# A second softmax taken in halves in every step, in a kernel whose whole order is a table

## The chip, the cores and the metric

The kernel runs on one core of a Trainium2 chip, in float32. The metric is the device time of one execution in microseconds (us). Five kinds of engine share the work: PE (TensorE, matrix products; PEld is its loading of weights), DVE (VectorE), ACT (ScalarE), POOL (GpSimd) and SP (SyncE, which here issues every transfer). Sixteen DMA engines move data between the chip's memory (HBM) and the on-chip buffers.

## The reference, cut to what matters

```python
# q, k, v: (8 batches, 8 heads, 576, 64); p: (8, 8, 32, 64)
def sm_attn(qq, kk, vv):
    s = scale * np.matmul(qq, kk.transpose(0, 1, 3, 2))
    a = np.exp(s - np.max(s, axis=-1, keepdims=True))
    a = a / (np.sum(a, axis=-1, keepdims=True) + 1e-09)
    return np.matmul(a, vv)
p_packed = sm_attn(p, k, v)               # first softmax, over 576 keys
x = sm_attn(q, p_packed, p_packed)        # second softmax, over 32 pack rows
# x becomes (4608 tokens, 512); phi: (512, 32 slots); w1: (8, 512, 1024); w2: (8, 1024, 512)
logits = x @ phi
d = softmax(logits over tokens);  slot_input = d.T @ x       # 8 experts x 4 slots
slot_out[e] = np.maximum(slot_input[e] @ w1[e], 0.0) @ w2[e]
c = softmax(logits over slots);   out = c @ slot_out
```

## The kernel before, in words

**Steps.** The attention is done in 8 steps: step i holds one pair of batches (dd = i // 2) and one half of the heads (g = i % 2, four heads). A step goes from the scores of the pack queries (s1) through the first softmax (mx1, e1), its transposes (ap, copied by apc), the product with v (m, scaled by ppa and pp), the transpose of the result (pt, copied by ptc), the product with phi (mp, copied by mm), the transposes of q (qp, copied by qc), the second scores (s2), the second softmax (mx2 the maximum over 32 pack rows, sb the subtraction, e2 the exponential, z2 the sum, rc the reciprocal of the sum, n2 the normalisation) and the transposes of its probabilities (a2p, copied by a2c) to the routing logits (lg). kt is DVE's 32x32 transposition of k. Names that begin with f and g, and rt, rb, gt, gs, sa, keep a running softmax over tokens and gather the slot inputs after every second step. Then come the experts' two layers (weights streamed from HBM) and the output, whose 36 tiles of 128 tokens are stored as they are made: the first 16 tiles by left and right halves of their 512 columns, the others whole.

**Order.** Nothing is scheduled by itself: a long string, ORDER, lists tokens `name.i.j@bank:engine` (step i, part j, PSUM bank, a for ACT, v for DVE, p for POOL), and each token calls the function f_name. Every engine works its instructions off in that order. A transfer's place on SP's queue follows from it too.

**Parts of the second softmax.** The scores of a step are two halves by the parity of the head (576 of 1152 elements per partition each). `mx2.i.2` and `sb.i.2` take both halves at once, `mx2.i.0` and `.1` one; e2, z2, rc and n2 take part 0 (all), 6 or 7 (one parity). On DVE z2 is one reduction; on POOL it is one addition and two shorter ones, and rc then begins with a short reduction on DVE. Before the change steps 0 to 5 use the whole and steps 6 and 7 halves.

**Loads.** All loads are issued by SP in one fixed list into a ring of 30 x 4096 bytes per partition. ALLOW holds them back: the load of index ALLOW[k] waits until 194 + 256 k products' worth of PE work is done (a product counts 4, a transpose 2; a pause of PE's counter, not of time). The load of a late chunk of weights, the only one into the tile `a` (PLACE's letter "x"), waits for the end of the attention, and the ring's later loads wait for the first expert layer to free their places.

**Stores.** `ends_a` lists after which left-half tiles a transfer is sent:

```python
    def tiles(t0, t1, x):
        ...
            ends = (ends_a, ends_b)[x]
            if t + 1 in ends:
                send(max(n for n in (0, *ends) if n <= t), t + 1, x)
```

Of the kernel before, what the change touches and what calls it, by code (L numbers as in the profile page):

```python
# [34 lines left out]
a2p.0.1@3 a2c.0.0:a rz.2.0 kt.3.3 ap.2.2@2 e2.1.0 ap.2.0@0 apc.2.2:v s1.3.0@4 a2c.0.1:a z2.1.0:p
s1.3.1 apc.2.0:a a2c.0.2:a m.2.0@2 mx1.3.0 m.2.1 m.2.2 e1.3.0 rc.1.0 e1.3.1 lg.0.0@1 n2.1.0:v
ppa.2.1 ap.3.1@0 ra.3.0 ap.3.0@7 ppa.2.0 apc.3.1:a ap.3.2@6 pp.2.1 apc.3.0:a a2p.1.2@5 kt.4.1
a2p.1.0@0 a2c.1.2:a apc.3.2:v a2p.1.1@7 a2c.1.0:a rz.3.0 m.3.0@4 pp.2.0 a2c.1.1:a kt.4.3 lg.0.1
kt.4.2 pt.2.0 f1.0.0 m.3.1 ptc.2.1:a ptc.2.0:a kt.4.0 f2.0.0 m.3.2 f3.0.0 f5.0.0 mp.2.0 fd.0.0
ppa.3.1 f6.0.0 mm.2.0:v ppa.3.0 pp.3.1 gr.0.0@6 pp.3.0 gz.0.0 fl.0.0 s2.2.0@1 rt.0.1:v rt.0.0:a  # L40
s2.2.1 qp.3.2@0 mx2.2.2 pt.3.0 qc.3.2:a gt.0.0 ptc.3.1:a ptc.3.0:v qp.3.5@0 rb.0.0 sb.2.2 mp.3.0
qc.3.5:a gs.0.0 mm.3.0:a qp.3.1@0 qp.3.3@5 qc.3.1:a sa.0.0 e2.2.0 qp.3.0@4 qp.3.4@7 qc.3.0:v
s1.4.0@0 qc.3.3:a z2.2.0:p s1.4.1 qc.3.4:a kt.5.0 kt.5.2 s2.3.0@5 mx1.4.0 s2.3.1 kt.5.1 e1.4.1
qp.4.5@4 mx2.3.2 e1.4.0 qc.4.5:a ap.4.2@0 ra.4.0 rc.2.0 qp.4.3@1 apc.4.2:a ap.4.1@4 sb.3.2 n2.2.0:p
qc.4.3:a qp.4.1@3 ap.4.0@0 apc.4.1:a qp.4.4@2 qp.4.2@1 qc.4.1:a qc.4.4:a kt.5.3 e2.3.0 s1.5.0@4
rz.4.0 apc.4.0:v s1.5.1 qc.4.2:a kt.6.0 z2.3.0:p a2p.2.0@0 mx1.5.0 a2p.2.2@1 a2c.2.0:a m.4.0@2
# [1207 lines left out]
```

## Time and profile before

| | before |
|---|---|
| median of 3 runs | 198.3 us (197.76 to 199.04) |
| the profiled execution | 198.95 us |
| its span | 196.8 us |
| PE busy | 167.2 us (85%) |
| DVE busy | 124.1 us (63%) |
| ACT busy | 89.7 us (46%) |
| POOL busy | 35.7 us (18%) |
| HBM read, written | 62.46 MB, 9.44 MB |

The span is the time from the first to the last event of the profiled execution; the 2.15 us by which the execution is longer lie around it. The attention's eight steps fill the first 135 us, the experts' weights and products the stretch to 167 us, the output the rest. Transfers run from the first microseconds to the end.

### The profile page before, as it was taken

How to read it: one execution, taken by the hardware profiler on the slowest of the kernel's cores; microseconds unless marked ns; L12 is line 12 of the kernel's file. 1: busy time of each engine (PE TensorE's matmuls, PEld its weight loads, DVE VectorE, ACT ScalarE, POOL GpSimd, SP SyncE). 2: the span in 40 equal slices, each digit the busy share in tenths (PEclk: the TensorE clock that was granted, in tenths of full speed). 3: DMA queues.
4: the chain of work that ended last, by engine and by line, in shares of the span. 5: the costliest groups of instructions: out<-in, count | busy, mean ns of one | idle time of the engine just before them, and what ended most of it. 6: DMA issues, size and time to landing. Idle time of an engine off the chain costs nothing.

```text
span 196.8 us, 6563 instructions
## 1 busy us (share of the span) xinstructions
PE 167.2 (85%) x2841; PEld 108.9 (55%) x2841; DVE 124.1 (63%) x261; ACT 89.7 (46%) x229; POOL 35.7 (18%) x61
## 2 busy tenths in 40 slices
PE   7978986999999999999999989687999997979100
PEld 4454574786777778597797867433333232448000
DVE  1657639797848999969746899745575111569300
ACT  4084273696526589575357367322021001459300
POOL 7400000544000572000403670403000000000000
PEclk9999999999999999999999999999999999999955
DMA  5999999699999999999999999999999999699995
GB/s 182 377 388 284 388 395 371 214 358 383 390 367 387 394 392 375 354 351 411 410 407 406 342 407 414 417 421 397 382 425 420 399 350 348 205 341 341 441 420 244
DMA packets 29228, 72.31 MB, mean 367 GB/s; under 512 B 2192, under 2 KB 10896, under 8 KB 27408
## 3 DMA queue, kind: packets, MB, share of 16 engines
q1 hardware_dynamic: 29200, 71.90, 97.3%
q8 instruction: 22, 0.36, 0.7%
q14 instruction: 6, 0.05, 0.1%
HBM read 62.46 MB, written 9.44 MB: 365 GB/s over the span
## 4 chain that ended last, share of the span: by engine, by line
PE 34%; DVE 25%; DMA 17%; ACT 9%; issue 3%; SPq 3%; POOL 1%; DVEq 0%; ACTq 0%; POOLq 0%
PE ps L150 31%; DMA ring<-in_k_dram 10%; DMA ring<-in_moe_w_dram 4%; DVE work L448 4%; ACT work L397 4%; PE ps L153 4%; DMA ring<-in_q_dram 3%; DVE work L401 3%; DVE mx L656 3%; SPq L159 3%; DVE ring L401 2%; ACT work L480 2%; DVE nm L477 1%; DVE work L666 1%; DVE zs L716 1%
## 5 line engine op out<-in xcount | busy, mean ns | idle before, releaser
L397 ACT COPY work<-ps 128x512 f32<-128x512 f32 (+3 forms) x68 | 30.0, 487 | 21.7 <-PE ps L153 18.3
L150 PE MATMUL ps<-work 128*64 128x64 f32 (+1 forms) x1088 | 34.0, 313 | 1.7 <-ACT work L397 0.7
L150 PEld LDWEIGHTS ps<-work 128*64 128x64 f32 (+1 forms) x1088 | 24.1, 122 | 10.0 <-issue 2.5
L448 DVE STREAM_TRANSPOSE work<-ring 128x576 f32<-128x576 f32 x32 | 23.3, 755 | 5.9 <-DMA ring<-in_k_dram 5.7
L153 PE MATMUL ps<-ident,ring 128*128 128x128 f32 x144 | 20.6, 280 | 0.1
L150 PE MATMUL ps<-ring,work 64*64 64x128 f32 x576 | 18.3, 273 | 2.2 <-issue 2.0
L150 PEld LDWEIGHTS ps<-ring,work 64*64 64x64 f32 x576 | 15.7, 133 | 4.8 <-issue 3.8
L397 ACT COPY a2Tb<-ps 128x384 f32<-128x384 f32 x21 | 9.8, 497 | 16.5 <-PE ps L153 16.3
L153 PEld LDWEIGHTS ps<-ident,ring 128*128 128x128 f32 x144 | 15.9, 141 | 2.5 <-DVE work L401 0.7
L480 ACT ACTIVATE work<-ps,nm 128x576 f32<-128x576 f32 x16 | 11.8, 739 | 11.9 <-DVE nm L477 11.8
L153 PE MATMUL ps<-ident,work 128*128 128x128 f32 x108 | 15.3, 279 | 1.9 <-ACT work L480 1.5
L656 DVE TENSOR_REDUCE mx<-ps 128x36 f32<-128x1152 f32 (+1 forms) x10 | 11.0, 1100 | 7.5 <-PE ps L150 7.5
L150 PE MATMUL ps<-a,a2Tb 32*128 32x256 f32 (+2 forms) x112 | 13.6, 505 | 2.0 <-DVE a2Tb L401 1.3
L401 DVE COPY ring<-ps 128x256 f32<-128x256 f32 (+1 forms) x25 | 11.3, 514 | 5.7 <-PE ps L150 5.6
L153 PEld LDWEIGHTS ps<-ident,work 128*128 128x128 f32 x108 | 11.8, 141 | 4.9 <-ACT work L480 3.4
L150 PE MATMUL ps<-ring,hT 128*32 128x512 f32 (+1 forms) x136 | 13.2, 496 | 0.3
L397 ACT COPY ring<-ps 128x256 f32<-128x256 f32 (+1 forms) x27 | 10.6, 483 | 5.9 <-PE ps L150 5.9
L150 PE MATMUL ps<-ones 128*128 128x512 f32 (+2 forms) x24 | 12.1, 615 | 1.0 <-DVE ones L118 1.0
L401 DVE COPY work<-ps 128x384 f32<-128x384 f32 (+3 forms) x24 | 11.5, 484 | 2.2 <-PE ps L153 1.8
L150 PE MATMUL ps<-ring,a2Tb 128*32 128x512 f32 x96 | 12.4, 594 | 0.4 <-DVE a2Tb L1076 0.4
L477 DVE TENSOR_REDUCE nm<-ps 128x2 f32<-128x1152 f32 x8 | 10.8, 1349 | 2.6 <-PE ps L150 2.6
L703 POOL TENSOR_TENSOR zt<-work 128x576 f32<-128x576 f32 x3 | 4.3, 1417 | 38.4 <-ACT work L695 38.4
(126 smaller groups left out, 218.1 us busy)
## 6 DMA issues: line engine op xcount, KB each, us to landing
ring<-in_moe_w_dram SPq DMA_DIRECT2D x22, 1024.0 KB, 9.3
ring<-in_k_dram SPq DMA_DIRECT2D x16, 576.0 KB, 8.6
ring<-in_q_dram SPq DMA_DIRECT2D x16, 576.0 KB, 6.7
ring<-in_v_dram SPq DMA_DIRECT2D x16, 576.0 KB, 7.9
work<-in_moe_w_dram SPq DMA_DIRECT2D x6, 1024.0 KB, 12.2
out_dram<-ring SPq DMA_DIRECT2D x2, 2304.0 KB, 10.5
ring<-in_moe_w_dram SPq DMA_DIRECT2D x3, 512.0 KB, 17.9
out_dram<-ring SPq DMA_DIRECT2D x2, 640.0 KB, 4.8
```

The source lines that it names most:

```text
L150: return step(nc.tensor.matmul(*a, **k), 4)
L153: return step(nc.tensor.transpose(*a, **k), 2)
L159: x = nc.sync.dma_start(out=dst, in_=src).ins
L397: nc.scalar.copy(dst, src)
L401: nc.vector.tensor_copy(dst, src)
L448: nc.vector.transpose(kT[:, b2, :, c].rearrange("p m (t r) -> p m t r", t=T), view(f"k{i}.{b2}").rearrange("p (m t c d) -> p m t c d", m=2 ...
L477: nc.vector.tensor_reduce(nms[i % 2], s1v(i), axis=AX.XY, op=ALU.max, negate=True)
L480: nc.scalar.activation(a1[:, :, x].rearrange("p t (h r) -> p h t r", h=2), s1v(i)[:, x].rearrange("p h (t r) -> p h t r", t=T), AF.Exp, bi ...
L656: nc.vector.tensor_reduce(mxs[i % 2][:, a0:a1].rearrange("p a t -> p (a t)"), s2v(i, j).rearrange("p a t s -> p (a t) s"), axis=AX.X, op=A ...
L666: nc.vector.tensor_tensor(a2s[i // NG % 2][:, :, i % NG, a0:a1].rearrange("p t a s -> p a t s"), s2v(i, j), mxs[i % 2][:, a0:a1].unsqueeze ...
L703: nc.gpsimd.tensor_tensor(y, a[:, :, :, 0:w], a[:, :, :, w:NS], op=ALU.add)
L716: nc.vector.reciprocal(z, z)
```

## The change

All eight steps take the second softmax in halves, the whole ORDER is another, ALLOW has other numbers, and the left halves of tiles 4 to 8 leave in three transfers (tiles 4 and 5, 6 and 7, 8) where one carried all five. ORDER has 585 tokens where it had 549. mx2, sb, e2 and rc are 16 tokens each where they were 10; z2 goes from 6 on POOL and 4 on DVE to 11 and 5, n2 from 7 and 3 to 9 and 7. Some copies out of PSUM go from ACT to DVE: qc on DVE 20 times where it was 10 (512 wide 12 where 5, 128 wide 8 as against 5), apc 10 where 8, a2c 8 where 4, rt 3 where 2, and mm once where 4. The dummy products (`w`) are 37 units both times. In the changed file line numbers above L24 are higher by 3 (L656 becomes L659).

```diff
-ALLOW = (24, 24, 24, 27, 31, 34, 39, 43, 47, 51, 55, 57, 60, 62, 64, 66)
+ALLOW = (24, 24, 24, 28, 32, 36, 40, 44, 48, 53, 56, 58, 61, 63, 65, 67)
...
-kt.2.1 ap.1.1@7 qp.1.3@6 apc.1.1:a mx2.0.2 qp.1.0@5 ap.1.0@7 qc.1.0:a ap.1.2@4 qc.1.3:v apc.1.0:a
+apc.1.1:a rz.1.0 mp.0.0 sb.0.1 apc.1.0:a ap.1.2@0 mm.0.0:a e2.0.7 s2.0.0@6 apc.1.2:v kt.2.0 z2.0.7:p
+qp.1.2@0 mx2.0.0 qp.1.4@5 qp.1.5@4 qc.1.2:a kt.2.1 qp.1.0@3 qc.1.5:a sb.0.0 qp.1.3@0 qc.1.0:a
...
-    ends_a = (1, 2, 4, 9, 12, 16)
+    ends_a = (1, 2, 4, 6, 8, 9, 12, 16)
```

**Place 1: DVE, where step 2's k arrives.** The L448 (L451) rows are the four transposes of step 2's k; mx_171 is the maximum of step 0's second softmax, rzm_170 and pp_153 belong to step 1. Before:

```order
L538 RECIPROCAL rzm_170<-rzm_170 128x4
L448 STREAM_TRANSPOSE work<-ring 128x2x288
L656 TENSOR_REDUCE mx_171<-ps 128x36
L401 COPY work<-ps 128x512
L448 STREAM_TRANSPOSE work<-ring 128x2x288 x3
L666 TENSOR_TENSOR work<-ps,mx_171 128x4x9x32
L547 SCALAR_TENSOR_TENSOR pp_153<-ps,rzm_170,pt_151 128x128 x2
```

Now:

```order
L659 TENSOR_REDUCE mx_171<-ps 128x18
L541 RECIPROCAL rzm_170<-rzm_170 128x4
L669 TENSOR_TENSOR work<-ps,mx_171 128x2x9x32
L404 COPY work<-ps 128x384
L451 STREAM_TRANSPOSE work<-ring 128x2x288
L659 TENSOR_REDUCE mx_171<-ps 128x18
L451 STREAM_TRANSPOSE work<-ring 128x2x288
L669 TENSOR_TENSOR work<-ps,mx_171 128x2x9x32
L451 STREAM_TRANSPOSE work<-ring 128x2x288 x2
L404 COPY work<-ps 128x128
```

One half's maximum and subtraction now stand ahead of the first transpose of step 2's k; the other half's stand among the four.

**Place 2: PE, from step 2's first scores on.** 32x288 with `work` on both sides is s1 of step 2, pp_1_153 the transpose pt of step 1, phi_sb the product mp, 64x64 is s2 of step 1, ident with `work` a transpose of probabilities, ident with `ring` one of q. Before:

```order
L150 MATMUL ps_75<-work_150 32x288 x16
L153 MATMUL ps_75<-ident_104,pp_1_153 128x128 x2
L150 MATMUL ps_75<-work_150 32x288 x16
L150 MATMUL ps_75<-phi_sb_79,work_150 64x32 x4
L150 MATMUL ps_75<-ones_77 128x128
L150 MATMUL ps_75<-work_150 64x64 x36
L153 MATMUL ps_75<-ident_104,ring_76 128x128 x9
```

Now:

```order
L153 MATMUL ps_75<-work_150 32x288 x32
L156 MATMUL ps_75<-ident_104,pp_1_153 128x128 x2
L156 MATMUL ps_75<-ident_104,work_150 128x128 x6
L153 MATMUL ps_75<-phi_sb_79,work_150 64x32 x4
L156 MATMUL ps_75<-ident_104,work_150 128x128 x3
L153 MATMUL ps_75<-work_150 64x64 x18
L156 MATMUL ps_75<-ident_104,work_150 128x128 x9
L153 MATMUL ps_75<-a2Tb_110,mm_0_156 32x288 x4
```

The transposes of step 0's second probabilities (a2p, the x6 and x3) now follow s1 at once, and only one half of s2 of step 1 stands there; the first logits (a2Tb with mm_0) follow soon after. The transposes of q, which stood next before, come later.

**Place 3: DVE, the last step's second softmax.** mx_1_172 and zs_1_174 are its maximum and sum, a2_1_109 its probabilities, zt POOL's partial sums. Before:

```order
L656 TENSOR_REDUCE mx_1_172<-ps_75 128x18
L807 STREAM_TRANSPOSE d_162<-rt_163 128x288
L666 TENSOR_TENSOR a2_1_109<-ps_75,mx_1_172 128x2x9x32
L812 STREAM_TRANSPOSE L_sb_136<-ps_75 128x288
L700 TENSOR_REDUCE zs_1_174<-a2_1_109 128x9x2 x2
L715 TENSOR_SCALAR zs_1_174<-zs_1_174 128x9x2
L716 RECIPROCAL zs_1_174<-zs_1_174 128x9x2
L715 TENSOR_SCALAR zs_1_174<-zs_1_174 128x9x2
L716 RECIPROCAL zs_1_174<-zs_1_174 128x9x2
L401 COPY a2Tb_110<-ps_75 128x384
L720 TENSOR_TENSOR a2_1_109<-a2_1_109,zs_1_174 128x9x64
```

Now:

```order
L659 TENSOR_REDUCE mx_1_172<-ps_75 128x18
L838 TENSOR_TENSOR z_run_147<-z_run_147,ps_75 128x32
L840 TENSOR_TENSOR z_run_147<-z_run_147,ps_75 128x32
L849 TENSOR_TENSOR S_run_148<-S_run_148,ps_75 128x128
L669 TENSOR_TENSOR a2_1_109<-ps_75,mx_1_172 128x2x9x32
L815 STREAM_TRANSPOSE L_sb_136<-ps_75 128x288
L717 TENSOR_REDUCE zs_1_174<-zt_159 128x9x2
L718 TENSOR_SCALAR zs_1_174<-zs_1_174 128x9x2
L719 RECIPROCAL zs_1_174<-zs_1_174 128x9x2
L703 TENSOR_REDUCE zs_1_174<-a2_1_109 128x9x2
L718 TENSOR_SCALAR zs_1_174<-zs_1_174 128x9x2
L719 RECIPROCAL zs_1_174<-zs_1_174 128x9x2
```

The first half's sum and normalisation are now POOL's (z2.7.6 and n2.7.6), the second half's are DVE's; on PE the two halves of s2 of step 7 stand back to back, where a product of the running softmax (f2.2) stood between them.

## Rows read from the trace of the kernel before

**Rows 1.** The page, parts 1 and 3: busy engines, the transfer queue.

```profile
PE 167.2 (85%) x2841; PEld 108.9 (55%) x2841; DVE 124.1 (63%) x261; ACT 89.7 (46%) x229; POOL 35.7 (18%) x61
...
q1 hardware_dynamic: 29200, 71.90, 97.3%
```

**Rows 2.** Busy time by stretch: stretch, its length, five engines, PEclk, DMA share, GB/s.

```profile
core 0: us, PE busy (x) PEld busy (x) DVE busy (x) ACT busy (x) POOL busy (x), PEclk, DMA share, GB/s
34.00:39.00 5.00, 4.71 (x149) 3.31 (x125) 3.78 (x8) 3.26 (x8) 2.70 (x3) 1.00 0.65 207
37.00:118.00 81.00, 78.06 (x1662) 61.50 (x1658) 65.69 (x128) 50.97 (x132) 23.96 (x23) 1.00 1.01 381
70.00:80.00 10.00, 9.76 (x234) 7.11 (x233) 9.93 (x19) 8.24 (x22) 4.83 (x4) 1.00 1.05 385
136.00:164.00 28.00, 27.85 (x274) 9.40 (x274) 11.87 (x32) 3.79 (x8) 1.37 (x1) 1.00 1.03 392
137.00:139.00 2.00, 2.00 (x24) 0.63 (x18) 1.67 (x5) 0.19 (x1) 0.37 (x1) 1.00 1.01 342
168.00:172.00 4.00, 4.00 (x53) 1.84 (x53) 2.26 (x6) 1.46 (x5) 0.00 (x0) 1.00 0.53 178
172.00:182.00 10.00, 8.56 (x80) 6.38 (x77) 7.82 (x18) 7.42 (x20) 0.00 (x0) 1.00 1.03 341
```

**Rows 3.** Timeline of SP's queue: start, length, instruction, and how many in a row.

```profile
34.70 0.37 SPq L159 DMA_DIRECT2D ring<-in_k_dram  x1
...
133.00 0.38 SPq L159 DMA_DIRECT2D a<-in_moe_w_dram  x1
...
136.99 3.40 SPq L159 DMA_DIRECT2D ring<-in_moe_w_dram  x5
```

**Rows 4.** Timeline of DVE and PE, step 2's k; last [idle before <-releaser].

```profile
27.88 0.78 DVE L448 STREAM_TRANSPOSE work<-ring 128x576 f32<-128x576 f32 x1 [2.33 <-DMA ring<-in_k_dram]
28.58 1.32 DVE L656 TENSOR_REDUCE mx<-ps 128x36 f32<-128x1152 f32 x1
...
30.42 2.08 DVE L448 STREAM_TRANSPOSE work<-ring 128x576 f32<-128x576 f32 x3
...
32.42 1.32 DVE L666 TENSOR_TENSOR work<-ps,mx 128x1152 f32<-128x1152 f32 x1
...
33.80 0.78 PE L150 MATMUL ps<-work 32*32 32x288 f32 x32 [0.63 <-DVE work L666]
```

**Rows 5.** Groups by line and shape: busy us, mean ns | idle before, releasers.

```profile
L656 DVE TENSOR_REDUCE mx<-ps 128x36 f32<-128x1152 f32 x6 | 8.0, 1341 | 4.9 <-PE ps L150 4.9
L656 DVE TENSOR_REDUCE mx<-ps 128x18 f32<-128x576 f32 x4 | 3.0, 739 | 2.7 <-PE ps L150 2.7
L666 DVE TENSOR_TENSOR a<-ps,mx 128x576 f32<-128x576 f32 x4 | 2.9, 742 | 0.0
L401 DVE COPY work<-ps 128x512 f32<-128x512 f32 x5 | 3.4, 673 | 0.7 <-PE ps L153 0.7
L401 DVE COPY a2Tb<-ps 128x384 f32<-128x384 f32 x6 | 3.2, 535 | 8.3 <-PE ps L153 8.3
L477 DVE TENSOR_REDUCE nm<-ps 128x2 f32<-128x1152 f32 x8 | 10.8, 1349 | 2.6 <-PE ps L150 2.6
L716 DVE RECIPROCAL zs<-zs 128x18 f32<-128x18 f32 x4 | 1.1, 266 | 0.1
L720 POOL TENSOR_TENSOR a<-a,zs 128x576 f32<-128x576 f32 x3 | 3.5, 1167 | 6.1 <-DVE zs L715 5.7 <-DVE zs L716 0.4
```

**Rows 6.** Timeline, last step: second scores, normalisation, last logits.

```profile
118.48 1.27 PE L150 MATMUL ps<-work 128*64 128x64 f32 x36
...
124.32 1.27 DVE L720 TENSOR_TENSOR a<-a,zs 128x576 f32<-128x576 f32 x1
...
127.59 0.69 PE L150 MATMUL ps<-a2Tb,mm 128*32 128x288 f32 x8 [0.30 <-ACT a2Tb L397]
```

**Rows 7.** Timeline of ACT and DVE where the left output halves are copied.

```profile
167.56 1.64 DVE L401 COPY ring<-ps 128x256 f32<-128x256 f32 x4 [2.04 <-PE ps L150]
...
170.40 0.65 ACT L397 COPY ring<-ps 128x256 f32<-128x256 f32 x2 [1.35 <-PE ps L150]
```

More of the change, by code (lines that the diff above doesn't have):

```diff
@@ L35 @@
[L35 to L46, printed above, removed]
@@ new lines @@
+qp.1.1@4 kt.2.3 qc.1.3:a m.1.0@1 e2.0.6 kt.2.2 m.1.1 qc.1.1:a qc.1.4:v z2.0.6:p m.1.2 rc.0.7
+s1.2.0@4 ppa.1.1 ppa.1.0 pp.1.1 s1.2.1 pp.1.0 n2.0.7:p rc.0.6 n2.0.6:v pt.1.0 ptc.1.0:a ptc.1.1:v
+a2p.0.2@0 mx1.2.0 a2p.0.0@3 mp.1.0 a2c.0.0:a mm.1.0:a a2p.0.1@3 a2c.0.2:v e1.2.1 s2.1.0@1 kt.3.1
+e1.2.0 kt.3.0 ra.2.0 ap.2.0@0 a2c.0.1:v ap.2.1@7 apc.2.0:v ap.2.2@6 apc.2.1:v lg.0.0@3 apc.2.2:a
+kt.3.3 m.2.0@4 rz.2.0 mx2.1.0 m.2.1 kt.3.2 m.2.2 sb.1.0 s2.1.1@6 ppa.2.1 ppa.2.0 pp.2.1 e2.1.6
+pp.2.0 z2.1.6:p qp.2.1@2 mx2.1.1 pt.2.0 qp.2.3@1 ptc.2.0:a ptc.2.1:v qp.2.4@0 sb.1.1 mp.2.0 qc.2.4:a
@@ new lines @@
+qp.2.0@0 mm.2.0:a qc.2.3:v e2.1.7 s1.3.0@4 rc.1.6 qc.2.0:a z2.1.7:v s1.3.1 n2.1.6:p qc.2.1:v rc.1.7
+qp.2.2@0 mx1.3.0 n2.1.7:p qp.2.5@2 qc.2.2:a qc.2.5:a kt.4.1 a2p.1.0@0 e1.3.0 s2.2.1@1 kt.4.2
+a2c.1.0:a e1.3.1 kt.4.0 a2p.1.2@0 ra.3.0 mx2.2.1 ap.3.1@7 a2c.1.2:a ap.3.2@6 apc.3.1:v ap.3.0@5
+apc.3.2:a sb.2.1 a2p.1.1@4 apc.3.0:a s2.2.0@6 a2c.1.1:v e2.2.7 rz.3.0 kt.4.3 z2.2.7:p qp.3.5@4
+mx2.2.0 qp.3.3@5 qc.3.5:a qp.3.1@2 sb.2.0 qp.3.2@1 qc.3.3:a qp.3.4@0 qc.3.1:a rc.2.7 lg.0.1 qc.3.2:a
+qc.3.4:a n2.2.7:p s1.4.0@4 e2.2.6 f1.0.0 s1.4.1 kt.5.0 z2.2.6:p m.3.0@0 mx1.4.0 m.3.1 rc.2.6 m.3.2
@@ new lines @@
+e1.6.0 lg.1.1 kt.7.2 ppa.5.0 ra.6.0 ap.6.2@7 ppa.5.1 pp.5.0 ap.6.0@3 f1.1.0 a2p.4.0@2 apc.6.0:a
+apc.6.2:v ap.6.1@1 a2c.4.0:a pp.5.1 a2p.4.1@0 apc.6.1:a rz.6.0 a2p.4.2@7 kt.7.1 a2c.4.1:a pt.5.0
+a2c.4.2:a f2.1.0 ptc.5.0:v s1.7.0@0 ptc.5.1:a f3.1.0 f5.1.0 s1.7.1 late.0.0 late.1.0 fd.1.0 lg.2.0@7
+mx1.7.0 mp.5.0 f6.1.0 mm.5.0:a gr.1.0@5 e1.7.0 fl.1.0 gz.1.0 e1.7.1 ra.7.0 s2.5.1@0 rt.1.1:v
+rt.1.0:a rz.7.0 gt.1.0 mx2.5.1 s2.5.0@2 rb.1.0 sb.5.1 e2.5.7 gs.1.0 mx2.5.0 qp.6.3@4 sa.1.0 z2.5.7:p
+qp.6.4@1 sb.5.0 qp.6.0@0 qc.6.3:a qp.6.5@6 qc.6.4:a qc.6.0:a m.6.0@4 qc.6.5:v e2.5.6 rc.5.7 ap.7.0@0
@@ new lines @@
+z2.5.6:p qp.6.1@6 n2.5.7:v apc.7.0:a m.6.1 m.6.2 qc.6.1:v ap.7.2@0 ppa.6.0 rc.5.6 ppa.6.1 qp.6.2@6
+pp.6.0 apc.7.2:a pp.6.1 ap.7.1@3 qc.6.2:v pt.6.0 m.7.0@0 apc.7.1:v ptc.6.0:a ptc.6.1:v m.7.1
+late.2.0 n2.5.6:v s2.6.1@2 mp.6.0 mx2.6.1 m.7.2 mm.6.0:a sb.6.1 a2p.5.2@6 ppa.7.1 ppa.7.0 pp.7.1
+a2p.5.0@2 e2.6.7 a2c.5.2:v a2p.5.1@3 a2c.5.0:a pp.7.0 s2.6.0@4 z2.6.7:v a2c.5.1:a rc.6.7 qp.7.2@6
+mx2.6.0 n2.6.7:p qp.7.4@3 qp.7.5@2 qc.7.2:a qc.7.4:v sb.6.0 lg.2.1 qc.7.5:v qp.7.0@6 e2.6.6 pt.7.0
+f1.2.0 qp.7.3@2 z2.6.6:p ptc.7.1:a qc.7.0:v ptc.7.0:a f2.2.0 qc.7.3:a qp.7.1@5 f3.2.0 mp.7.0
@@ new lines @@
+qc.7.1:v f5.2.0 s2.7.0@5 mm.7.0:v fd.2.0 rc.6.6 s2.7.1@0 late.3.0 mx2.7.0 n2.6.6:p sb.7.0 f6.2.0
+a2p.6.1@2 mx2.7.1 e2.7.6 gr.2.0@5 late.4.0 late.5.0 gz.2.0 a2c.6.1:a z2.7.6:p sb.7.1 a2p.6.2@4
+fl.2.0 rt.2.0:a a2p.6.0@0 e2.7.7 rc.7.6 a2c.6.2:a z2.7.7:v a2c.6.0:a n2.7.6:p rt.2.1:a lg.3.0@7
+rc.7.7 gt.2.0 n2.7.7:v xz.0.0 w.1.0@4 rb.2.0 a2p.7.2@0 a2p.7.1@4 a2c.7.2:a a2p.7.0@3 a2c.7.1:v
+gs.2.0 a2c.7.0:a sa.2.0 lg.3.1 w.3.0@6 f1.3.0 f2.3.0 w.4.0@6 f3.3.0 f5.3.0 fd.3.0 f6.3.0 gr.3.0@5
+lx.0.0 fl.3.0 gz.3.0 w.3.0@4 rt.3.0:a rt.3.1:a gt.3.0 rb.3.0 gs.3.0
```

50 lines of the change are left out of this document (17 added, 33 removed).

## The prediction, made before the changed kernel ran

> **What bounds the kernel now.** I read the page's busy shares first, then the stretches, then the timeline where a stretch has a hole. No engine is busy for the whole span: PE for 85%, DVE 63%, the transfer queue 97.3% [rows 1]. The stretches tell what that means: transfers run at a share of 1.01 to 1.05 through the attention and through the experts, with two holes that matter, 34 to 39 us (share 0.65, so 5 x 0.35 = 1.75 us lost) and 168 to 172 us (0.53, so 4 x 0.47 = 1.9 us) [rows 2]. In the attention PE is as full: 78.06 of 81 us between 37 and 118 us, 27.85 of 28 in the first expert layer [rows 2]. So two things bind together. The attention's end sets when the late loads start: the one into `a` is issued at 133.00 us and five into the ring at 136.99 us [rows 3], and at 137 to 139 us the queue is full with a share of 1.01 [rows 2], with no slack seen. From this follows the rule that I use: an attention that ends later by Y makes the kernel later by Y; one that ends earlier by Y helps only as far as the loads come earlier too, that is up to the 1.75 us lost at 34 to 39 us.
>
> **The change, part by part.**
>
> *DVE at step 2's k.* Before, DVE idles 2.33 us until k lands and transposes it from 27.88 us; the whole maximum (1.32 us), a copy and the whole subtraction (1.32 us) come after, and the first scores of step 2 start on PE at 33.80 us, released by that subtraction's end [rows 4]. Now one half of the maximum and the subtraction stands ahead of the first transpose, in the idle 2.33 us, and costs nothing. What is left from 27.88 us on is 0.78 + 2.08 us of transposes [rows 4], half a maximum of 0.74 and half a subtraction of 0.74 [rows 5], some 4.3 us, so the scores may start at about 32.5 us with the hand-over to PE: **-1.3 us**. Bounds: nothing (k itself late) to -1.5.
>
> *PE behind it.* Step 2's scores last 2 x 0.78 us, to about 34.1 us by that sum. Next on PE now stand the transposes of step 0's second probabilities, and these wait for a normalisation on DVE, which stands behind two reciprocals, two scalings and 0.74 (like the half subtraction [rows 5]) to 1.27 us (the one half that DVE normalises now [rows 6]) of its own: about 35.0 to 35.6 us, so PE waits 0.6 to 1.2 us. On DVE that normalisation is also ahead of step 2's first maximum (1.35 us [rows 5]), which PE's transposes of step 2 wait for, as before. I take the lead as nearly spent: **+1.2 us**, between 0 and +1.3. Queued behind the waiting transposes on PE are mp and the second scores of step 1, whose copies and maxima wait in turn.
>
> *The middle.* DVE gets more work. Halving: six steps x (2 x 0.739 - 1.341 = 0.14 for the maximum; 2 x 0.742 - 1.32 = 0.16 for the subtraction [rows 4, 5]) is 1.8 us; a second addition and reciprocal in six steps, at most 0.27 us each [rows 5] and less for what the whole one shrinks, taken as 2 us. Copies from ACT: 7 of 512 columns x 0.673 us is 4.7, 4 of a2c x 0.535 us is 2.1 [rows 5], the narrow ones about 1.8 more by the same rate. In all some 12 us, of which about 10 fall between 37 and 118 us. DVE idles 81 - 65.69 = 15.3 us there [rows 2]. From below: between 70 and 80 us DVE was busy 9.93 of 10 us and PE still 9.76 [rows 2], so a full DVE alone costs PE next to nothing: 0; and below nothing, since smaller pieces reach PE sooner, down to closing half of PE's 81 - 78.06 = 2.94 idle us, -1.5. From above: 65.69 + 10 + 2 is 77.7 us, and if the waits of the maxima for PE (4.9 and 2.6 us [rows 5]) stay, 85.2 us against 81: +4.2. I take **+0.5 us**, nearest to the stretch at 70 to 80 us, which is the one with DVE as full as the new order makes it.
>
> *The last step.* From the end of its second scores (118.48 + 1.27 = 119.75 us) to the end of the last logits (127.59 + 0.69 = 128.28 us) [rows 6] it takes 8.53 us. Exponentials, transposes, copies and logits are the same; the second half's normalisation stays on DVE and no longer stands behind the first half's small steps (0.27 us of reciprocal [rows 5]), and takes 0.74 instead of 1.27 us if POOL has finished the first half (1.17 us [rows 5]) by then. The two halves of the second scores also follow each other without the softmax product between. Together **-0.6 us**, between -0.2 and -1.4; if POOL is late, its reductions are what comes last and it is 0.
>
> So the attention ends about 0.2 us earlier (-1.3 + 1.2 + 0.5 - 0.6).
>
> *ALLOW.* One load of step 3's k, which waited for products and left at 34.70 us [rows 3], is no longer the one held: the next is. It can follow the loads ahead of it and fill most of the 1.75 us hole. That puts every later load earlier, but alone it is worth nothing: the load into `a` and those behind it wait for the attention's end. Where the higher numbers admit later the same holds; SP has queued behind each gate only loads until the stores. Bounds 0 to -1.75; taken 0 beyond the 0.2 us above.
>
> *Stores.* The left halves of tiles 4 to 7 are copied by 167.56 + 1.64 = 169.2 us, that of tile 8 by about 170.7 us [rows 7], and all five leave then. Now four tiles of 131 KB leave from about 169 us, in the hole at 168 to 172 us [rows 2]; at 341 GB/s [rows 2] they take 524 / 341 = 1.5 us, which the hole covers. What follows is made no earlier: the copies of the later tiles set when later stores start, so the queue can run empty later instead. Two more issues on SP cost about 0.37 us each [rows 3], with the next stores behind them. Bounds -1.5 to +0.8; taken **-0.4 us**, since at 172 to 182 us the queue is full at 1.03 [rows 2] and what has left it by then is in part gained.
>
> The Trainium skill, "DMA: Bandwidth & Descriptors", section "Measured (HBM→SBUF, 128 partitions, SWDGE, issued from GpSimd)", speaks against this edit: it wants transfers of at least 1 MiB and has 256 KB pieces well below full rate. By it the sum would have no -0.4, and the third rival below would be the likely one; the stretch from 172 to 182 us [rows 2], full with such stores, does not bear it out.
>
> **The sum.** -0.2 - 0.4 = -0.6 us. The profiled execution took 198.95 us, which becomes 198.35; the median of the runs lies 0.65 below the profiled one, so **197.7 us**.
>
> **The rivals.**
>
> *Faster.* The middle costs nothing or less, the lead at step 2 is kept, and the attention ends 1.75 us or more earlier; the hole at 34 to 39 us is filled, so the loads can follow. 198.3 - 1.75 - 0.4 = **196.2 us**, and 195.1 with all of -1.5 for the stores. For it: the stretch at 70 to 80 us, and that waits of DVE for PE (4.9 + 2.6 us [rows 5]) are room that halves can use. Against it: PE has only 2.94 us of idle time between 37 and 118 us [rows 2], and much of that is the start of its products.
>
> *Slower: DVE becomes the bound of the middle.* The 10 us do not fit into 15.3, since DVE's idle time is waiting for scores. PE then waits for copies of q, through one buffer, and for the maxima. The middle costs +4.2 in place of +0.5: 197.7 + 3.7 = **201.4 us**. It decides from where the counterpart of the 81 us has DVE busy for more than about 78 us; at +2.6 or more the kernel is over 1% slower. For it: more of normalising on DVE goes beside POOL, which took 1.27 us for a half where a like operation took 0.74 [rows 5, 6]. The Trainium skill, "GPSIMD Engine Reference", section "Specifications", says that GpSimd shares its SBUF interfaces with VectorE and contends with instructions that have two SBUF inputs; the 1.27 us beside POOL agree. Against it: only 7 normalisations are on DVE.
>
> *The split stores cost.* Two issues and smaller pieces, with no gain: +0.8 in place of -0.4: **198.9 us**.
>
> *The change doesn't do what it says.* The first two of the split stores leave no earlier than the one before, since on ACT and DVE the copies of tiles 4 to 7 are late or SP is still issuing; the halves meet the same waits as the whole, and DVE's lead at k is lost because k lands late. Then -0.2 at most: **198.1 us**.
>
> **How the numbers follow.** About 1%, 2 us, is what a measurement of this kernel can tell from no change: 196.3 and 200.3 are the limits. Forecast 0.40, with 197.0 to 199.5 as its own range; faster 0.26; DVE bound 0.19; split stores cost 0.08; not what it says 0.07. Within 1% are the forecast and the last two: 0.55. The range leaves out a tenth at each side: from 195.3, inside the faster case near its end of 195.1, to 201.4, the price of the DVE bound.
>
> **What would show it.** Right: step 2's first scores start near 32.5 us and the maximum of step 2 near its old place; the hole at 34 to 39 us is gone; DVE is busy some 75 us between the same two points of the middle with PE at 77 to 78; the last logits end about 128 us; the left stores of tiles 4 to 7 leave before 170 us. Wrong: PE idle before the transposes of probabilities (a2p) or of q for several us, a normalisation on DVE of 1.2 us many times over, or an end of the attention before 134 or after 138 us. An attention that ends much earlier while the late loads don't would refute the rule of the first part.

## The result and the profile after

The changed kernel takes 201.44 us (median of 6 runs, 201.04 to 204.23) where the kernel before, run beside it, takes 198.08 us (6 runs). The ratio is 1.015, with a 95% interval of 1.0107 to 1.0192; it leaves out one slow run (204.23 us), so it lies a little under the ratio of the medians. Run again later, the changed kernel came to 1.0177 (1.0125 to 1.023). It is slower by some 3 us where the forecast's sum had 0.6 us less.

The profiled execution took 201.09 us with a span of 199.3 us. The page of the changed kernel, parts 1 and 3, answers to [rows 1]:

```profile
PE 167.8 (84%) x2841; PEld 109.2 (55%) x2841; DVE 140.0 (70%) x309; ACT 84.8 (43%) x221; POOL 37.3 (19%) x78
...
q1 hardware_dynamic: 29232, 71.90, 96.3%
```

PE and the transfers do the same work; DVE has 16 us more, ACT 5 less. The stretches of the changed kernel, with the columns of [rows 2]:

```profile
34.00:39.00 5.00, 3.83 (x61) 3.28 (x62) 4.94 (x8) 2.63 (x8) 0.00 (x0) 1.00 1.05 390
37.00:118.00 81.00, 74.87 (x1615) 58.60 (x1610) 74.01 (x157) 45.79 (x124) 19.29 (x28) 1.00 1.00 370
136.00:164.00 28.00, 26.95 (x274) 9.25 (x266) 12.58 (x36) 3.58 (x8) 1.83 (x1) 1.00 0.95 361
137.00:139.00 2.00, 1.02 (x24) 0.77 (x24) 0.71 (x3) 0.00 (x0) 0.32 (x1) 1.00 0.88 246
168.00:172.00 4.00, 2.96 (x26) 1.67 (x30) 1.82 (x5) 1.67 (x5) 0.00 (x0) 1.00 0.95 302
```

The hole in the transfers at 34 to 39 us is gone (share 1.05), as forecast, but between 37 and 118 us PE is busy 3.2 us less than before, and at 137 to 139 us, where the queue had been full, it is not. What the late loads wait for comes later; the timeline of SP's queue, against [rows 3]:

```profile
136.16 0.38 SPq L162 DMA_DIRECT2D a<-in_moe_w_dram  x1
140.14 0.33 SPq L162 DMA_DIRECT2D ring<-in_moe_w_dram  x1
```

Both are 3.15 us later, and so is the attention's end. The end of the last second scores is at 121.59 us against 119.75 (+1.84), the end of the last logits at 131.43 against 128.28 (+3.15): more than half of the loss is there before the last step's softmax, the rest (1.31 us) within it. The timeline of that last part, PE, POOL and DVE (start, length, engine, line, [idle before <-releaser]), answers to [rows 6]:

```profile
119.27 2.32 PE L153 MATMUL ps<-work 128*64 128x64 f32 x72
...
125.63 1.17 POOL L723 TENSOR_TENSOR a<-a,zs 128x576 f32<-128x576 f32 x1 [0.85 <-DVE zs L719]
...
126.20 1.55 DVE L718 TENSOR_SCALAR zs<-zs 128x18 f32<-128x18 f32 x1
...
126.74 0.98 POOL L983 MEMSET a2Tb<- 128x1056 f32 x1
...
127.78 0.27 DVE L719 RECIPROCAL zs<-zs 128x18 f32<-128x18 f32 x1
128.08 0.76 DVE L723 TENSOR_TENSOR a<-a,zs 128x576 f32<-128x576 f32 x1
...
128.99 1.18 PE L156 MATMUL ps<-ident,a 128*128 128x128 f32 x9 [1.51 <-DVE a L723]
...
130.73 0.69 PE L153 MATMUL ps<-a2Tb,mm 128*32 128x288 f32 x8 [0.19 <-ACT a2Tb L400]
```

Look at the row at 126.20 us: the addition of 1e-9 to 18 sums per partition takes 1.55 us. Other runs of the same operation take 0.11 to 0.18 us. It starts while POOL normalises the first half (to 126.80 us) and ends when POOL's next instruction, the clearing of a2Tb, ends (127.72 us). Behind it wait the reciprocal, the second half's normalisation, and PE (1.51 us). The groups by line and shape of the changed kernel show that this is no single case; they answer to the reciprocal's row of [rows 5]:

```profile
L718 DVE TENSOR_SCALAR zs<-zs 128x18 f32<-128x18 f32 x16 | 5.7, 356 | 0.5
...
L719 DVE RECIPROCAL zs<-zs 128x18 f32<-128x18 f32 x16 | 4.3, 267 | 0.5
```

The 16 additions cost 5.7 us, twice what they need; the four long ones are 0.82 us (at 32.72 us), 0.56 (47.36), 0.78 (104.59) and 1.55 us (126.20), each ending within 0.05 us of an instruction of POOL's. The reciprocals keep their 0.27 us. And these are the waits of PE of over 1 us between 24 and 110 us, from its timeline:

```profile
34.77 0.85 PE L156 MATMUL ps<-ident,work 128*128 128x128 f32 x6 [1.26 <-DVE work L723]
...
49.59 0.55 PE L156 MATMUL ps<-ident,work 128*128 128x128 f32 x3 [1.33 <-POOL work L723]
...
102.88 0.82 PE L156 MATMUL ps<-ident,ring 128*128 128x128 f32 x6 [1.74 <-issue]
```

Two are transposes of second probabilities (a2p) that wait for a normalisation; for the third see the last section.

### The profile page after: what moved, and what is told of

The parts are those of the page before. It is cut to its first block, busy times and chain, and to the rows that moved or that the text cites. A ratio compares the mean times of both kernels' runs of the same rounds, so it can differ in the third digit from the quotient of the medians.

```text
span 199.3 us, 6633 instructions
## 1 busy us (share of the span) xinstructions
PE 167.8 (84%) x2841; PEld 109.2 (55%) x2841; DVE 140.0 (70%) x309; ACT 84.8 (43%) x221; POOL 37.3 (19%) x78
## 4 chain that ended last, share of the span: by engine, by line
PE 45%; DVE 28%; ACT 7%; issue 6%; DMA 4%; SPq 2%; POOL 1%; DVEq 0%; ACTq 0%; POOLq 0%
PE ps L153 35%; PE ps L156 10%; DMA ring<-in_moe_w_dram 4%; DVE work L404 4%; DVE nm L480 3%; DVE work L451 3%; ACT work L483 3%; DVE mx L659 3%; DVE zs L718 2%; DVE ring L404 2%; DVE a L669 2%; SPq L162 2%; DVE zs L719 2%; DVE zs L703 1%; ACT work L400 1%
## 5 line engine op out<-in xcount | busy, mean ns | idle before, releaser
L400 ACT COPY work<-ps 128x512 f32<-128x512 f32 (+3 forms) x56 | 24.5, 479 | 22.8 <-PE ps L156 18.4
L153 PE MATMUL ps<-work 128*64 128x64 f32 (+1 forms) x1088 | 33.2, 313 | 0.9 <-DVE work L404 0.6
L451 DVE STREAM_TRANSPOSE work<-ring 128x576 f32<-128x576 f32 x32 | 23.4, 754 | 2.0 <-DMA ring<-in_k_dram 1.9
L404 DVE COPY work<-ps 128x512 f32<-128x512 f32 (+3 forms) x36 | 17.6, 508 | 2.8 <-PE ps L156 2.3
L156 PEld LDWEIGHTS ps<-ident,ring 128*128 128x128 f32 x144 | 15.9, 141 | 6.6 <-issue 3.0
L156 PE MATMUL ps<-ident,work 128*128 128x128 f32 x108 | 15.8, 281 | 3.7 <-POOL work L723 1.3
L400 ACT COPY a2Tb<-ps 128x384 f32<-128x384 f32 x17 | 7.9, 485 | 19.2 <-PE ps L156 19.2
L706 POOL TENSOR_TENSOR zt<-work 128x288 f32<-128x288 f32 x6 | 4.8, 800 | 58.5 <-ACT work L698 58.5
L659 DVE TENSOR_REDUCE mx<-ps 128x18 f32<-128x576 f32 x16 | 11.9, 745 | 3.0 <-PE ps L153 2.8
L153 PE MATMUL ps<-ones 128*128 128x512 f32 (+2 forms) x24 | 12.6, 645 | 1.1 <-DVE ones L121 1.1
```

The source lines that it names most:

```text
L153: return step(nc.tensor.matmul(*a, **k), 4)
L156: return step(nc.tensor.transpose(*a, **k), 2)
L400: nc.scalar.copy(dst, src)
L404: nc.vector.tensor_copy(dst, src)
L451: nc.vector.transpose(kT[:, b2, :, c].rearrange("p m (t r) -> p m t r", t=T), view(f"k{i}.{b2}").rearrange("p (m t c d) -> p m t c d", m=2 ...
L659: nc.vector.tensor_reduce(mxs[i % 2][:, a0:a1].rearrange("p a t -> p (a t)"), s2v(i, j).rearrange("p a t s -> p (a t) s"), axis=AX.X, op=A ...
```

## The experiments

Each was timed beside the kernel before; "ratio" is to that kernel, with its 95% interval. The theories: **A**, PE stands at transposes that wait for a normalisation, and in the last step POOL's instructions hold up DVE; **B**, DVE's added work bounds the middle; **C**, the transfers cost the time. Theory **D**, formed after the first eight runs, is that DVE's small addition stands still while POOL works, everywhere.

**The clearing of a2Tb later.** The clearing is made to wait for the last normalisation.

```diff
-        nc.gpsimd.memset(a2Tf[:, 0 : E * XZ], 0.0)
+        x = nc.gpsimd.memset(a2Tf[:, 0 : E * XZ], 0.0).ins
+        tc.add_manual_dep(x, state["n2"], ...)   # the last normalisation
```

> The changed kernel, with POOL's clearing of a2Tb made to wait for the last step's last normalisation; all the rest as in the changed kernel. Theory A (PE stands at transposes that wait for a normalisation, and in the last step POOL's instructions hold up DVE): the addition of the last half's sum, 1.55 us at 126.20 us in the changed kernel, is held only by POOL's normalisation to 126.8 us and not by the clearing behind it to 127.7, so it takes about 0.6 us; the attention ends about 0.95 us earlier and the kernel takes 0.8 to 1.0 us less than the changed one's 201.1, about 200.2 us. Theory B (DVE's added work bounds the middle): the addition is slow for another reason, and the time stays at 201.1 us.

Ratio 1.010 (1.005 to 1.015), 200.41 us. DVE's and POOL's timeline in this run:

```profile
124.93 1.17 POOL L723 TENSOR_TENSOR a<-a,zs 128x576 f32<-128x576 f32 x1 [0.85 <-DVE zs L719]
125.50 0.63 DVE L718 TENSOR_SCALAR zs<-zs 128x18 f32<-128x18 f32 x1
...
127.37 0.98 POOL L984 MEMSET a2Tb<- 128x1056 f32 x1 [1.27 <-DVE a L723]
```

The addition now ends with POOL's normalisation, after 0.63 us, as A said; from the end of the last second scores to the end of the last logits it takes 8.91 us in place of 9.84. The time fell by about 1 us, though its interval and that of the changed kernel (1.0107 to 1.0192) overlap.

**The three stores alone**, on the kernel before.

```diff
-    ends_a = (1, 2, 4, 9, 12, 16)
+    ends_a = (1, 2, 4, 6, 8, 9, 12, 16)
```

> The kernel before, with the left halves of tiles 4 to 8 stored in three transfers; nothing else. The prediction's term: 0.4 us less, between 1.5 less and 0.8 more, so 197.7 us beside 198.1. Theory C (the transfers, not the attention, made the changed kernel slower): 0.5 to 1.5 us more.

Ratio 0.9947 (0.9918 to 0.9976): 1.05 us less, the right sign and over twice the 0.4 us taken. C is wrong as to the stores.

**Copies back on ACT**, in the changed kernel.

```diff
-qc.0.2:v ... qc.0.0:v ... apc.0.2:v ... a2c.0.2:v
+qc.0.2:a ... qc.0.0:a ... apc.0.2:a ... a2c.0.2:a
(each copy on the engine that it had before)
```

> The changed kernel, with every copy out of PSUM on the engine on which the kernel before had it, which takes some 7 us of copies from DVE and gives them to ACT; order and halves stay. Theory B (DVE bounds the middle): DVE catches up, the second scores of the last step end up to 1.85 us earlier, and the kernel takes 199.3 to 200 us. Theory A: the order was made for the other engines, the transposes go on waiting for their normalisations, and the time is within 0.7 us of 201.1 us.

Ratio 1.0253 (1.0198 to 1.0308): 2.0 us more than the changed kernel (1.5 by its later run), which neither theory foresaw. Taking this work from DVE gained nothing, so the copies that the change moved to DVE are not what cost the time; in this order they pay.

**Halves alone**, in the order of the kernel before.

```diff
-mx2.0.2 ... sb.0.2 ... e2.0.0 ... z2.0.0:p ... rc.0.0 ... n2.0.0:p
+mx2.0.0 mx2.0.1 ... sb.0.0 sb.0.1 ... e2.0.6 e2.0.7 ... z2.0.6:p z2.0.7:p ... rc.0.6 rc.0.7 ... n2.0.6:p n2.0.7:p
(and so in steps 1 to 5)
```

> The kernel before with its own order, each whole operation of the second softmax in steps 0 to 5 (maximum, subtraction, exponential, sum, reciprocal, normalisation) split in place into its two halves, on the same engine. This adds some 4 us to DVE and nothing else. Theory A: halves by themselves cost PE little, since DVE has idle time in the middle and the first half may start earlier: within 0.5 us of 198.1 us. Theory B: 4 us of added DVE work, a third of what the change adds, cost a third of the loss or more: 199 us or more.

Ratio 1.0107 (1.0071 to 1.0143): 2.1 us more. A, as I had it, is wrong here and B's number is right. But the trace shows how; POOL, DVE and PE in this run:

```profile
111.00 1.17 POOL L723 TENSOR_TENSOR work<-work,zs 128x576 f32<-128x576 f32 x1 [0.95 <-DVE zs L717]
111.04 1.16 DVE L718 TENSOR_SCALAR zs<-zs 128x18 f32<-128x18 f32 x1
...
113.83 0.66 PE L156 MATMUL ps<-ident,ring 128*128 128x128 f32 x4 [1.32 <-DVE a L669]
```

The first half's reciprocal sets POOL to its normalisation, and the second half's addition, which DVE starts 0.04 us later, takes as long as POOL's instruction. PE waits 1.32 us for the subtraction that stands behind it on DVE. With wholes the addition comes before POOL starts (the six of 128x36 in the kernel before take 0.18 us each); it is the second half that runs into the first. This is theory D. From step 7's first scores to the end of the last second scores it takes 27.40 us here, with this addition on the way, and 25.7 to 26.3 us in the traces of the kernel before, of the stores alone and of the new ALLOW alone; from step 2's first scores to step 3's, with another addition of 1.16 us at 38.40 us, it takes 10.69 us against 9.6 us in those three.

**Old stores and old ALLOW**, in the changed kernel.

```diff
-    ends_a = (1, 2, 4, 6, 8, 9, 12, 16)
+    ends_a = (1, 2, 4, 9, 12, 16)
-ALLOW = (24, 24, 24, 28, 32, 36, 40, 44, 48, 53, 56, 58, 61, 63, 65, 67)
+ALLOW = (24, 24, 24, 27, 31, 34, 39, 43, 47, 51, 55, 57, 60, 62, 64, 66)
```

> The changed kernel with the stores (ends_a) and the load gates (ALLOW) of the kernel before; the new order and the halves stay. Theory C (the transfers cost the time): back to within 0.7 us of 198.1 us. Theories A and B (the attention ends later for reasons of its own): 201.1 us or a little more, up to 201.9, since the hole in the transfers around 36 us comes back.

Ratio 1.0226 (1.0163 to 1.0289), no gain: C is not the cause. (The upper end of A and B, 201.9 us, is a ratio of 1.019, within the interval.)

**Two transposes later**, in the changed kernel.

```diff
-n2.0.6:v pt.1.0 ptc.1.0:a ptc.1.1:v a2p.0.2@0 mx1.2.0 a2p.0.0@3 mp.1.0 ... s2.1.0@1
+pt.1.0 ptc.1.0:a ptc.1.1:v mx1.2.0 n2.0.6:v mp.1.0 mm.1.0:a s2.1.0@1 a2p.0.2@0 a2p.0.0@3
-a2p.1.0@0 e1.3.0 s2.2.1@1
+e1.3.0 s2.2.1@1 a2p.1.0@0
```

> The changed kernel with two pieces of its order turned round: step 2's first maximum and step 1's second scores now stand ahead of step 0's second normalisation on DVE and of its transposes on PE, and step 2's second scores ahead of step 1's transposes. Theory A (PE stands at transposes that wait for a normalisation, 1.26 us at 34.8 us and 1.33 us at 49.6 us): both waits go, PE is 1 to 2 us ahead at 50 us, and the kernel takes 0.5 to 2 us less than 201.1 us. Theory B (DVE bounds the middle): DVE has as much to do, the lead is lost by 118 us, and the time stays within 0.4 us of 201.1 us.

Ratio 1.022 (1.0177 to 1.0264), so no faster than the changed kernel (1.015 and 1.0177): A's gain did not come. The two waits fell to 0.64 us and none, but others came, of 1.04 us for a copy on DVE and 0.91 us for an exponential on ACT. Moving a wait to another place on PE did not shorten the whole.

**The new ALLOW alone**, on the kernel before (the ALLOW lines of the change).

> The kernel before with the changed kernel's ALLOW alone. The prediction's term: nothing by itself, within 0.4 us of 198.1 us, with the hole in the transfers at 34 to 39 us mostly filled. Theory C: 0.5 us more or worse, since loads admitted earlier take turns with others.

Ratio 1.0065 (1.0031 to 1.01): 1.3 us more. C's number, in a small part; the mechanism is not settled (below).

**The front**, on the kernel before, with both the new ALLOW and the new stores.

```diff
-kt.2.1 ... mx2.0.2 ... sb.0.2
+mx2.0.0 sb.0.0 kt.2.1 mx2.0.1 ... sb.0.1
(and step 0's e2, z2, rc, n2 in halves)
```

> The kernel before with three small pieces of the change: step 0's second softmax in halves, with the first half's maximum and subtraction ahead of the first transpose of step 2's k on DVE, the new ALLOW, and the stores in three transfers. The order is otherwise that of before. By the prediction's terms step 2's first scores start some 1.0 to 1.3 us earlier; if PE, which is full from there to 118 us, keeps that lead, the attention ends as much earlier and the kernel takes 196.6 to 197.4 us with 0.4 of the stores. Rival: the lead is spent by the next wait that is not moved (step 2's first maximum and k of step 3), and only the stores' share is left, 197.7 to 198.1 us.

Ratio 1.0059 (1.0018 to 1.0101). Step 2's first scores start at 31.93 us, 1.9 us earlier than before, and step 3's at 42.83, 0.6 us earlier: the lead is spent, partly at an addition that takes 1.16 us at 38.27 us beside POOL's normalisation. Against the run with the stores alone (32.60 and 42.20 us) it is 0.7 us earlier and then 0.6 us later.

**No addition**, in the changed kernel. This and the runs below leave out the addition of 1e-9 to the sums of the second softmax; each sum is at least 1.

```diff
-        nc.vector.tensor_scalar_add(z, z, EPS)
         nc.vector.reciprocal(z, z)
```

> The changed kernel without the addition of 1e-9 to the second softmax's sums (16 small operations on DVE; each sum is at least 1, so a reader may take the reciprocal as it stands). Theory D (DVE's small addition between two SBUF buffers stands still while POOL works, and the halves bring POOL's normalisation of one half against the addition of the other): its four stretched runs, 0.82 at 32.7, 0.56 at 47.4, 0.78 at 104.6 and 1.55 us at 126.2 us against 0.11 to 0.18, disappear, the reciprocals keep their 0.27 us, and the kernel takes 1.4 us or more less than the changed one, so a ratio of about 1.008 or under to the kernel before. Rival: whatever DVE does next is held up as long, the reciprocals then take 0.8 to 1.5 us, and the ratio stays at 1.013 to 1.015 less 0.002 for the work left out.

Ratio 0.9942 (0.9914 to 0.997), 197.02 us: 4.1 us less than the changed kernel, for 16 operations that need 2.9 us at the most. The two waits of PE at a2p in this run, and a normalisation on DVE ahead of the first:

```profile
33.16 1.09 DVE L722 TENSOR_TENSOR work<-work,zs 128x576 f32<-128x576 f32 x1
...
34.40 0.85 PE L156 MATMUL ps<-ident,work 128*128 128x128 f32 x6 [0.87 <-DVE work L722]
...
48.54 0.55 PE L156 MATMUL ps<-ident,work 128*128 128x128 f32 x3 [0.60 <-POOL work L722]
```

They were 1.26 and 1.33 us; the last step takes 8.20 us (119.23 to 127.43) in place of 9.84. The rival was wrong on the reciprocals, which take 0.21 to 0.27 us, but not wholly: DVE's normalisation, which needs 0.7 to 0.8 us, now starts earlier, beside POOL, and takes 1.09 us at 33.16, 1.70 at 71.10, 0.99 at 102.34 and 0.92 at 123.94 us, where in the changed kernel one of seven was stretched (1.50 us). The standing still has in part moved to the next operation that can be held.

**Halves without the addition**, in the order of the kernel before.

> The kernel before with all whole operations of the second softmax split in place into halves (as the earlier run at a ratio of 1.0107) and without the addition of 1e-9 to its sums. Theory D: the additions that took 1.16 us at 38.4 us and at 111.0 us are what made the halves cost 2.1 us, so most of that goes: a ratio of 1.000 to 1.004. Theory B (4 us more of work on DVE): the 16 additions left out are some 2.5 us of it, so about half of the cost stays at least, 1.005 to 1.007; if the reciprocals are held up in their place, 1.009 or more.

Ratio 0.9972 (0.9933 to 1.0012), against 1.0107 with it. That is under both theories' bounds, and nearest to D's, whose 1.000 is within the interval. The kernel before with wholes and without the addition came to 0.9975 (below), so the halves as such cost nothing that can be measured.

**The kernel before with the three stores and no addition.**

> The kernel before with the three stores and without the addition of 1e-9 to the second softmax's sums; wholes and order as before. The kernel before has two stretched additions (0.73 us at 113.7 and 0.31 at 116.2 us), both short before the last step. Theory D: 0.2 to 0.6 us less than with the three stores alone (a ratio of 0.9947), so 0.992 to 0.994, which would be the fastest of these kernels. Rival: those additions hide beside PE's work, 0.994 to 0.996.

Ratio 0.9925 (0.9891 to 0.9958), within D's bounds; the rival's are not excluded.

**The changed kernel with no addition and the later clearing.**

> The changed kernel without that addition and with POOL's clearing of a2Tb behind the last normalisation. Theory D: without the addition nothing stands before the clearing's end any more, so the later clearing gives nothing further beyond what the missing addition gave, within 0.4 us of it. Rival: the reciprocal takes the addition's place behind POOL, and the later clearing still gives 0.9 us.

Ratio 0.9946 (0.9914 to 0.9977), as without the later clearing: once the addition is gone, nothing waits for the clearing.

**A spare reciprocal in the addition's place**, to tell the holding up from the work.

```diff
-        nc.vector.tensor_scalar_add(z, z, EPS)
+        nc.vector.reciprocal(part(spare, c), z)
         nc.vector.reciprocal(z, z)
```

> The changed kernel with the addition of 1e-9 to the second softmax's sums replaced, in each of its 16 places, by a reciprocal of the same sums into a spare buffer that nobody reads: 0.26 us each, more work on DVE than the 0.18 us of an undisturbed addition, and an operation that was not held up in the run without additions. Theory D (holding up): within 0.6% of the run without the addition, a ratio of 0.994 to 1.000. Rival (it was the work): 1.012 to 1.018, as the changed kernel or slower.

Ratio 1.0098 (1.0067 to 1.013), between both theories' numbers. POOL and DVE in this run, at the place where the addition took 1.55 us:

```profile
125.26 1.17 POOL L724 TENSOR_TENSOR a<-a,zs 128x576 f32<-128x576 f32 x1 [0.94 <-DVE zs L720]
125.83 0.27 DVE L719 RECIPROCAL spare<-zs 128x18 f32<-128x18 f32 x1
126.13 0.27 DVE L720 RECIPROCAL zs<-zs 128x18 f32<-128x18 f32 x1
126.37 0.98 POOL L984 MEMSET a2Tb<- 128x1056 f32 x1
126.43 0.76 DVE L724 TENSOR_TENSOR a<-a,zs 128x576 f32<-128x576 f32 x1
```

Two reciprocals run beside POOL's normalisation without being held, and DVE's normalisation beside the clearing. So the addition's standing still is gone (one normalisation, 1.41 us at 72.72 us, is still stretched), and yet only part of the time came back: D alone is not the whole.

**The kernel before without the addition.**

> The kernel before without the addition of 1e-9 to the second softmax's sums (10 operations). Theory D: two of them were held up for some 0.8 us together, short before the last step; 0.2 to 0.8 us less, a ratio of 0.996 to 0.999. Rival (the addition costs by its number, not by being held): 10 of 16 of what the changed kernel gained by losing it, 4.1 x 10 / 16 = 2.6 us, a ratio of 0.987.

Ratio 0.9975 (0.9943 to 1.0008): at most a little, as D said, and not in proportion to the number of additions.

**No addition in the last step alone**, in the changed kernel.

```diff
+        if i < NSTEP - 1:
             nc.vector.tensor_scalar_add(z, z, EPS)
```

> The changed kernel without that addition in the last step alone. Theory D with the trace's lengths: the addition at 126.2 us took 1.55 in place of 0.18 us on the path to the attention's end, so 1.2 to 1.5 us less than the changed kernel, a ratio of 1.008; what is left to the run without any addition (0.994) then lies in the steps before. Rival: the last step is all of it, a ratio of 0.997 or less.

Ratio 1.0088 (1.0056 to 1.0121), as expected: some 1.2 to 1.8 us of the loss, by 1.015 or 1.0177, is the last step's held addition.

**The changed kernel again.**

> The changed kernel again, as it is, beside the three others: 1.011 to 1.019 if nothing but the neighbours' differences stands between these calls.

Ratio 1.0177 (1.0125 to 1.023).

**The spare reciprocals elsewhere.** No addition, and 16 reciprocals of the same size where nobody waits for them.

```diff
+        if c == 0:                       # in f_kt, behind the transposition of k
+            nc.vector.reciprocal(spare, ones[:, 0:18])
```

> The changed kernel without the addition of 1e-9 to the second softmax's sums, and with 16 spare reciprocals of the same size elsewhere on DVE: one behind every second transposition of k (read from the constant ones, written to a buffer that nobody reads). If DVE is simply full, it is as slow as with the spare reciprocal in the addition's place: 1.008 to 1.012. If the place between sum and normalisation is what counts, it is as fast as without: 0.993 to 0.999.

Ratio 0.9988 (0.9952 to 1.0024), against 1.0098 in the addition's place and 0.9942 without. The same work on DVE costs 2.2 us (1.1% of 198) more between a sum and its normalisation than elsewhere: it is the place, for the larger part. Set side by side, 5.7 us of additions in that place cost 4.1 us, and 4.1 us of spare reciprocals 3.1 us, in both cases about three quarters of the time that they take. So what counts there may be how long the place is taken, by work or by standing still; this is an estimate from the two runs, and no run varies that time alone.

**The best of the above on the kernel before**: three stores, no addition, step 0 in halves with its first half ahead of k, old ALLOW.

> The kernel before with the three stores, without the addition, and with step 0's second softmax alone in halves, the first half's maximum and subtraction ahead of the first transpose of step 2's k on DVE; the old ALLOW. In the earlier run of this front (ratio 1.0059, with the new ALLOW) step 2's first scores started 1.9 us earlier than before and lost most of it to an addition held 1.16 us by POOL at 38.3 us, which is gone here. If that lead lasts, 0.5 to 1.3 us less than the stores without the addition (0.9925), so 0.986 to 0.990; if the next wait takes it, 0.992 to 0.994.

Ratio 0.9862 (0.9803 to 0.992), the lowest of all and below both kernels; 196.67 us beside 198.11. Its interval overlaps that of the same without the front (0.9891 to 0.9958), and its trace has step 3's first scores at 42.00 us, no earlier than the 41.98 us of the kernel before without the addition. That the front adds to it is not shown.

## Why the prediction was wrong, point by point

**What bounds it** held in the main. Both late loads and the attention's end moved by the same 3.15 us. The span became 2.5 us longer (the profiled execution 2.14): some 0.6 us was made up behind the load into `a`, which is followed by 63.2 us where it was 63.8. That the stores did it is not shown: with the old stores in the changed kernel it is 63.1 us.

**DVE at step 2's k** held. The first scores start at 31.39 us, 2.4 us earlier than [rows 4], but about 1 us of that is k, which came earlier:

```profile
26.91 0.78 DVE L451 STREAM_TRANSPOSE work<-ring 128x576 f32<-128x576 f32 x1 [0.32 <-DMA ring<-in_k_dram]
...
31.39 1.75 PE L153 MATMUL ps<-work 32*32 32x288 f32 x64
```

From k's first transpose to the first scores it is 4.48 us, where the kernel before takes 5.92 us (from 27.88 us, and in the run with the stores alone from 26.68 to 32.60 us). So the order gave -1.4 us, for the term's -1.3.

**PE behind it** was right in mechanism: the forecast wait of 0.6 to 1.2 us is the 1.26 us at 34.77 us. The addition before that normalisation took 0.82 us, held up beside POOL, which the sum did not have; without the addition the wait is 0.87 us.

**The middle** was mis-sized. These three terms sum to +0.4 us; at the end of the last second scores +1.84 us was measured. The amount of DVE work between 37 and 118 us was near (74.01 us busy where I had some 75.7). Over the whole span it grew by 15.9 us where I had 12; the additions alone make 3.3 us of that (5.7 us, and 1.3 + 1.1 us before), for which, with the reciprocals, the working had 2. That a full DVE alone costs little agrees with the copies: taking them back gave nothing. What I took the price from, a stretch in which DVE was full and PE not hindered, was the wrong row, because the change adds operations to a chain on which PE waits: sum, addition, reciprocal, normalisation, once for each half in place of once. That this chain is the reason rests on one link of it: removing it gave the changed kernel 4.1 us and the kernel before about 0.5, by its interval perhaps nothing; reciprocals elsewhere on DVE cost 0.9 us, and in its place in the chain 3.1 us (0.9942 to 0.9988 and to 1.0098).

**The last step** is the term that failed: -0.6 us, with bounds of -0.2 to -1.4 us and 0 if POOL is late, against +1.31 us. Of the 3.35 us by which the attention's end was missed, 1.91 are here and 1.44 in the three terms before. My working took the small operations of both kernels as equal and looked for POOL's price only at normalisations on DVE. The addition of the second half, 1.55 us, was held by POOL's normalisation of the first and by the clearing behind it; the later clearing (8.91 us) and the missing addition (8.20 us) show it. The 8.20 us are 0.33 less than the 8.53 of before, within the term's bounds; but the kernel before without the addition takes 8.33 us in its trace, so what the new order itself gave is only some 0.1 us. A likely reason stands in place 3 of the listings: on DVE the second half does still stand behind the first half's small steps, against what the working says. They run from 124.81 to 125.56 us, and the second half's sum starts at 125.47 us, though the exponential that it needs ends at 124.98 us. POOL's being late was named, but not this: that POOL's working itself stops so small an operation on DVE.

The Trainium skill, "SBUF — State Buffer", section "SBUF: two separate sides", has the rule: DVE and GpSimd share a pair of ports, and whichever starts first, a GpSimd instruction or a DVE instruction in a two-port mode or with two SBUF inputs (these last only against a GpSimd instruction that reads SBUF), keeps it to its end. The additions that end with POOL's instruction (1.16 us beside 1.17) agree, and so does that DVE's normalisation, with its two inputs, is not held by the clearing (0.76 us beside 0.98), which reads nothing. In the prediction I used the rule for normalisations alone.

**ALLOW** was taken as 0 with bounds of 0 to -1.75 us and measured at +1.3 us by itself. The hole at 34 to 39 us was filled, as said. Why the kernel before then becomes slower stays open: in the one trace, step 2's first scores are at 33.91 us and the load into `a` at 133.32 us, 0.1 and 0.3 us later than before, which is less than what was timed. Against the trace of the stores alone, whose code is the same up to there as before, it is 1.3 and 2.0 us later; one trace of each cannot decide it.

**Stores**: -0.4 us taken, -1.05 us measured with the stores alone, within the bounds. The hole at 168 to 172 us is what they fill: its share is 0.99 in that run.

**The rivals.** The time of the slower one, 201.4 us, is what came, but not by its mechanism: DVE stayed below the 78 us from which it was to decide, and the copies, which it named as what PE waits for, are not it. The match is chance. What it had right is the argument that DVE's operations beside POOL take longer; it looked for it at normalisations, and the additions were hit. (Its +2.6 for over 1% slower does not come out of its sum: with +2.6 in place of +0.5 that gives 199.8 us, and 200.3 only with +3.1.) That the split stores cost is refuted by the run with the stores alone.

How the loss divides, by ratios: halves in the old order +1.07%, the new ALLOW +0.65%, the stores -0.53%, together +1.2% of the 1.5 to 1.8%. The rest is the new order and the moved copies, and within the intervals. But the parts need not add up: taking stores and ALLOW back together in the changed kernel should give -0.1% by these numbers, and gave +0.5 to 0.8%, though the intervals overlap. With the addition out of both, the changed kernel (0.9942) is no faster than the kernel before with the three stores alone (0.9925): halves, new order, moved copies and ALLOW together gained nothing that was measured.

## What to carry to other kernels

Splitting an operation in halves multiplies the small operations behind it; price each by whether the busiest engine waits behind that chain, not by the splitting engine's idle time. When POOL works beside DVE, look for short DVE operations that take far longer than their like and end with a POOL instruction: here a small addition that started second stood still and a reciprocal did not, and replacing the addition or leaving it out was worth more than the split. Measure the parts of a bundled change singly: here one part gained (the stores), two lost, and an 18-element addition made the difference between a loss of 1.5% and none.
